# Attention in units of half the sequence of a pair of heads, and a dense expert whose work starts after four units

## The chip, the cores and the metric

One core of a Trainium2 chip runs the whole program in one launch. The metric is device time in microseconds. The engines are TensorE (PE), VectorE (DVE), ScalarE (ACT), GpSimd (POOL) and SyncE (SP, which here issues DMAs alone). Before the change the median of three runs is 761.54 us (760.5 to 762.2).

## The reference

Two parts follow each other: block attention with sorted keys and values, then a dense mixture of eight experts over its output.

```python
# attention: B=4 batches, H=8 heads, S=768, D=64, 8 blocks of 96 positions
P = sort_net                                  # (B, H, 8, 8)
for _ in range(5):                            # a Sinkhorn iteration
    P = exp(P - max(P, -1)); P /= sum(P, -1) + 1e-9; P /= sum(P, -2) + 1e-9
k_sorted = einsum('bhij,bhjcd->bhicd', P, k_blocks)     # likewise v_sorted
scores = q_block @ k_sorted_block.T / 8       # each block of q sees one block of 96 keys
out = softmax(scores) @ v_sorted_block

# experts: x is (3072, 512), the heads side by side; 8 experts, F = 1024
P = exp(x @ w_gate - max)                     # (3072, 8)
for _ in range(8): P /= sum(P, 1); P /= sum(P, 0); P *= 3072 / 8
out = sum over e of P[:, e] * (relu(x @ w1[e]) @ w2[e])
```

All experts run on all tokens. The routing weights need every token's logits, and so the end of attention; an expert's own product `relu(x @ w1) @ w2` needs only the tokens that it is computed for.

## The kernel before

**Layout.** Matmul operands are bf16, sums f32 in PSUM. A pair of heads n (16 of them, four in a batch) is loaded by `load_pair` as three DMAs from POOL (k, v, q) into the tiles `kvr` and `qr`: each of the 128 partitions holds six neighbouring positions of both heads, so the partition is (block, CH = 16) and the six positions are CL. `relayout` (POOL; for pair 0 `relayout_part` on ACT) brings k and v of a position side by side, for the sort's weights.

**One unit of attention.** There are 32 units, one for each batch and head (NH = 32; unit g belongs to pair g // 2). The functions, which appear below with their lines, are:

- `q_transpose(n)` for a pair: six PE transposes of 128 columns, then four copies into `qT_`, two on DVE and two on ACT (the first two pairs: all four on ACT).
- `build_R` makes a unit's sort matrix R (128 x 8 x 16) from the Sinkhorn result `Pb`, on POOL for two units at a time.
- `sort_kv(g)`: six matmuls of 128 columns, one for each of the six positions in a partition, whose weights are k and v and whose moving operand is R; ACT copies the result to `kvT_` (three buffers), and SP issues a DMA transpose of v's half into `v1_`.
- `scores(g)`: eight matmuls of 96 columns, one for each block; DVE takes the maximum of each row (`mx`) and subtracts it (`ssb`).
- `weights(g)`: ACT's exp into `at_`. For units 16 to 29 (`DT`) a DMA transposes it into `aT_`; for the others `a_transpose` does, with eight PE transposes and a copy on ACT.
- `attend(g)`: eight matmuls of 65 columns (the 65th is the sum of the weights). `normalise(g)`: a reciprocal and a product on DVE, into `og_`.
- `x_transpose(n)` for a pair: eight PE transposes and a copy on ACT into `xtT`, the expert's input with features on the partitions.

`sort_kv`, `scores` and `attend` share two double-bank PSUM buffers (`psB`); the transposes and the expert pieces share four single banks (`psF`).

**Order.** The order of instructions is written out by hand; each engine works its own list in that order. A loop over steps s = 0 to 33 has, in each step: `scores(s)`, `a_transpose(s - 1)`, `sort_kv(s + 2)`, `weights(s)`, in even steps `q_transpose(s // 2 + 1)` and `relayout(s // 2 + 2)`, then any `x_transpose`, then `attend` and `normalise` of the unit before (of two units before, for those whose weights go by DMA), then `load_pair` by a table of steps.

**Expert 0 inside attention.** Between these, at four places in each step, `fill()` puts in pieces of expert 0: `l1_piece` (four matmuls of 384 columns and a Relu on ACT) and `l2_piece` (eight of 512 columns and a copy to the accumulator `osbl`, on DVE or, in one of three from chunk 2 on, ACT). A chunk is 384 tokens: eight l1 pieces and three l2 pieces. A list of slots spreads a batch's two chunks and its gate logits (`gate_piece`) over the calls that follow:

```python
        if new:
            add(new, {9:34,17:40,26:28}[s])
```

A batch is complete after its fourth pair's `x_transpose`, in steps 9, 17 and 26; the last batch's two chunks run after the loop, beside the routing. `load_expert(0)` (w1 and w2, two DMAs on POOL) stands at the end of step 2. Two buffers of `w1e` and two of `w2e` take turns; experts 1 to 7 run after the routing, 3072 tokens each, in groups of 512.

**After the loop** DVE works the routing's Sinkhorn iterations, beginning with the maximum `gmx`, while PE runs the remaining pieces of expert 0 and the first of expert 1, then experts 1 to 7.

Of the kernel before, what the change touches and what calls it, by code (L numbers as in the profile page):

```python
# [24 lines left out]
def kernel(  # L25
# [11 lines left out]
    nc = tc.nc  # L37
# [23 lines left out]
    rawp = ctx.enter_context(tc.tile_pool(name="rawp", bufs=6))  # L61
    iop = ctx.enter_context(tc.tile_pool(name="iop", bufs=2))
    raw_t, kv_t = {}, {}

# [9 lines left out]

    def relayout(n):

        kv = iop.tile([128, 2 * CL, 2, D], BF16, name="kv")
        nc.gpsimd.tensor_copy(kv.rearrange("p c t d -> p t c d"),  # L78
                              raw_t[n][0].rearrange("p t h c d -> p t (h c) d"))
        kv_t[n] = kv  # L80

    def relayout_part(n, e, t):

        if n not in kv_t:
            kv_t[n] = iop.tile([128, 2 * CL, 2, D], BF16, name="kv")
# [6 lines left out]
    load_pair(4)  # L92
# [15 lines left out]
    qT_ = perp.tile([128, 2, 2, S + 32], BF16)  # L108

    def zero_q(a):  # L110
        nc.scalar.copy(qT_[64:128, a].rearrange("p b c -> p (b c)"),
# [3 lines left out]
    nc.vector.memset(qT_[0:64, :, :, S:], 0.0)  # L115
# [45 lines left out]
    wp = ctx.enter_context(tc.tile_pool(name="wp", bufs=2))  # L161
    wg = ones.tile([128, 4, E], BF16)
    w1t, w2t = [], []

    def load_expert(e):
        w1e = wp.tile([128, 4, F], BF16, name="w1e")
        w2e = wp.tile([128, 8, Dm], BF16, name="w2e")
        nc.gpsimd.dma_start(out=w1e, in_=moe_w1[e].rearrange("(kk k) f -> k kk f", k=128))  # L168
        nc.gpsimd.dma_start(out=w2e, in_=moe_w2[e].rearrange("(fb k) f -> k fb f", k=128))
        w1t.append(w1e)  # L170
        w2t.append(w2e)
# [48 lines left out]
    def batch_pieces(b):  # L220

        out_ = []
        for c in (2 * b, 2 * b + 1):
# [29 lines left out]
    def q_transpose(n):  # L253


        qr = raw_t[n][1]
        tq = psF.tile([128, 2, CL // 2, 128], BF16, name="psF")
        for e in range(2):
            for c in range(CL // 2):
                nc.tensor.matmul(tq[:, e, c], qr[:, e, 2 * c:2 * c + 2].rearrange("p l d -> p (l d)"),  # L260
                                 Ibf, is_transpose=True, start=True, stop=True)
        for e in range(2):
            to = qT_[0:64, n % 2, e, 0:S].rearrange(
                "p (i c l h) -> p l c i h", i=NB, l=2, h=CH)
            for l in range(2):
                (nc.vector.tensor_copy if e == 0 and n > 1 else nc.scalar.copy)(  # L266
                    to[:, l], tq[64 * l:64 * l + 64, e].rearrange("p c (i h) -> p c i h", h=CH))

    q_transpose(0)
    q_transpose(1)  # L270


# [289 lines left out]
```

## Time and profile before

| | us |
|---|---|
| median of three runs | 761.54 (760.5 to 762.2) |
| the profiled execution, its own time | 760.26 |
| its span, first to last instruction | 758.5 |
| first sort of keys and values (step 0) | 14.23 |
| first matmul of expert 0 | 53.85 |
| `gmx`, the routing begins | 153.07 |

The span is what the profiler's page counts in; 1.8 us of the execution lie around it. "Busy" is the time in which an engine works on at least one instruction, "idle before" the time that it stood still just ahead of an instruction, with what released it. Matmul ends are modelled, so the spacing of starts tells more of PE than durations do. The mean granted clock of TensorE is 0.993 of full speed.

### The profile page before, as it was taken

The numbers are of one execution on the slowest core, as the hardware profiler recorded it, in microseconds if no ns is written. First come the engines' busy times: TensorE is split into PE (matmuls) and PEld (weight loads), VectorE is DVE, ScalarE is ACT, GpSimd is POOL, SyncE is SP. The second block draws the span as 40 slices with busy tenths as digits, with TensorE's granted clock in tenths as the row PEclk, the third lists the DMA queues.
The fourth block names the chain that finished last, engine by engine and source line by source line (L and its number), as shares of the span: only waits on it lengthen the run. The fifth ranks groups of instructions, "written<-read, shape, count | busy, mean of one in ns | idle before, by whom it ended". The sixth has DMA issues, their size and how long they took to land.

```text
span 758.5 us, 10311 instructions
## 1 busy us (share of the span) xinstructions
PE 725.8 (96%) x4274; PEld 367.7 (48%) x4340; DVE 268.3 (35%) x462; ACT 331.5 (44%) x559; POOL 80.6 (11%) x105
## 2 busy tenths in 40 slices
PE   2779999999999999999999999999999999999998
PEld 2566666654444444444444444444444444444444
DVE  5788787567422122121221221212212212112122
ACT  7888887653433423324324234243242342432422
POOL 8955420000000000000000000000000000000000
PEclk9979999999999999999999999999999999999999
DMA  9999744537000600033000700051001500002112
GB/s 152 191 179 173 101 92 83 80 51 111 1 1 0 102 10 1 0 53 59 0 1 1 111 1 1 0 81 31 0 1 29 83 0 1 1 0 98 70 69 98
DMA packets 58430, 40.14 MB, mean 53 GB/s; under 512 B 30608, under 2 KB 51344, under 8 KB 58384
## 3 DMA queue, kind: packets, MB, share of 16 engines
q0 software_dynamic: 26128, 26.23, 22.8%
q1 hardware_dynamic: 32256, 13.25, 8.4%
q8 instruction: 34, 0.56, 0.3%
q14 instruction: 12, 0.10, 0.0%
HBM read 52.45 MB, written 6.29 MB: 77 GB/s over the span
## 4 chain that ended last, share of the span: by engine, by line
PE 91%; ACT 3%; DVE 3%; DMA 1%; issue 1%; ACTq 0%; DVEq 0%
PE hps L445 38%; PE psF L523 38%; PE psF L203 5%; PE psF L192 5%; DMA v__108<-kvT__106 1%; PE psB L317 1%; PE psB L302 1%; ACT kvT__106 L305 1%; PE psB L346 1%; PE psF L339 1%; DVE ssb L324 1%; ACT at__114 L328 1%; DVE mx L322 0%; ACT qT__111 L266 0%; PE psF L364 0%
## 5 line engine op out<-in xcount | busy, mean ns | idle before, releaser
L448 ACT ACTIVATE hTs<-hps 128x512 bf16<-128x512 f32 x336 | 200.6, 597 | 372.9 <-PE hps L445 365.7
L445 PE MATMUL hps<-xtT,w1e 128*128 128x512 bf16 x1317 | 295.7, 379 | 1.5
L523 PE MATMUL psF<-w2e,hTs 128*128 128x512 bf16 (+1 forms) x1325 | 295.2, 378 | 1.4
L525 DVE SCALAR_TENSOR_TENSOR osbl<-psF,glog,osbl 128x512 f32<-128x512 f32 (+1 forms) x169 | 126.3, 747 | 437.6 <-PE psF L523 425.7
L523 PEld LDWEIGHTS <-hTs 128*128 128x128 bf16 x1352 | 132.2, 98 | 157.9
L445 PEld LDWEIGHTS <-w1e 128*128 128x128 bf16 x1344 | 131.6, 98 | 158.4
L192 PE MATMUL psF<-xtT,w1e 128*128 128x384 bf16 x256 | 49.0, 326 | 0.6 <-ACT qT__111 L266 0.6
L168 POOL DMA_DIRECT2D w1e<-in_moe_w_dram x8 | 6.1, 768 | 394.3 <-PE hps L445 370.4
L203 PE MATMUL psF<-w2e,hTs 128*128 128x512 bf16 x180 | 44.2, 379 | 0.6
L195 ACT ACTIVATE hTs<-psF 128x384 bf16<-128x384 f32 x64 | 29.7, 499 | 7.4 <-PE psF L192 6.8
L322 DVE TENSOR_REDUCE mx<-psB 96x8 f32<-96x768 f32 x32 | 30.4, 949 | 5.8 <-PE psB L317 5.4
L324 DVE TENSOR_TENSOR ssb<-psB,mx 96x768 f32<-96x768 f32 x32 | 30.5, 954 | 3.2
L305 ACT CAST kvT__106<-psB 128x768 bf16<-128x768 f32 x32 | 25.9, 809 | 11.6 <-issue 7.1
L192 PEld LDWEIGHTS <-w1e 128*128 128x128 bf16 x256 | 22.9, 98 | 12.7 <-issue 1.0
L328 ACT ACTIVATE at__114<-ssb 96x768 bf16<-96x768 f32 x32 | 27.3, 854 | 1.8 <-DVE ssb L324 1.8
L203 PEld LDWEIGHTS <-hTs 128*128 128x128 bf16 x192 | 17.8, 100 | 17.0
L78 POOL COPY kv<-kvr 128x1536 bf16<-128x1536 bf16 x15 | 22.0, 1468 | 30.5 <-issue 16.6
L355 DVE TENSOR_TENSOR og__236<-psB,den 96x512 bf16<-96x512 f32 x32 | 22.0, 686 | 1.1
L346 PE MATMUL psB<-v__108,aT__115 97*128 97x65 bf16 x256 | 13.6, 199 | 7.4 <-ACT kvT__106 L305 5.2
L302 PE MATMUL psB<-R,kv 128*128 128x128 bf16 x192 | 18.6, 242 | 1.9 <-ACT kvT__106 L305 0.9
L260 PE MATMUL psF<-Ibf,qr 128*128 128x128 bf16 x96 | 9.7, 248 | 11.0 <-DMA qr<-in_q_dram 11.0
L317 PE MATMUL psB<-kvT__106,qT__111 128*128 128x96 bf16 x256 | 18.0, 219 | 2.2 <-ACT kvT__106 L305 1.5
(82 smaller groups left out, 275.1 us busy)
## 6 DMA issues: line engine op xcount, KB each, us to landing
w1e<-in_moe_w_dram POOLq DMA_DIRECT2D x8, 1024.0 KB, 8.0
w2e<-in_moe_w_dram POOLq DMA_DIRECT2D x8, 1024.0 KB, 8.7
out_dram<-osbl SPq DMA_DIRECT2D x23, 256.0 KB, 2.0
kvr<-in_k_dram POOLq DMA_DIRECT2D x16, 192.0 KB, 7.6
kvr<-in_v_dram POOLq DMA_DIRECT2D x16, 192.0 KB, 7.6
qr<-in_q_dram POOLq DMA_DIRECT2D x16, 192.0 KB, 7.6
v__108<-kvT__106 SPq DMA_TRANSPOSE x32, 4.6
out_dram<-osbl SPq DMA_DIRECT2D x2, 128.0 KB, 1.7
```

The source lines that it names most:

```text
L192: nc.tensor.matmul(hps[:, 0:HC], w1t[0][:, kk, fb * 128:(fb + 1) * 128], xtT[:, kk, c * HC:(c + 1) * HC], start=(kk == 0), stop=(kk == 3))
L195: nc.scalar.activation(out=hT0[c][:, fb, 0:HC], in_=hps[:, 0:HC], func=AF.Relu)
L203: nc.tensor.matmul(oacc, hT0[c][:, fb, tt * 128:(tt + 1) * 128], w2t[0][:, fb, :], start=(fb == 0), stop=(fb == 7))
L302: nc.tensor.matmul(kvf[:, cl * 128:(cl + 1) * 128], kv[:, e * CL + cl].rearrange("p t d -> p (t d)"), R[:, g].rearrange("p i c -> p (i c)" ...
L305: nc.scalar.copy(kvT_[:, g % NKT, :, 0:96].rearrange("p i (l c) -> p i l c", c=CH), mkap(kvps, [kvps.ap[0], [CH, NB], [128, CL], [1, CH]]))
L322: nc.vector.reduce_max(out=mx, in_=s4, axis=AX.X)
L324: nc.vector.tensor_sub(ssb, s4, mkap(mx, [mx.ap[0], [4, 2], [1, 4], [0, 96]]))
L328: nc.scalar.activation(out=at_[:, g % NAT, :, 0:96], in_=ssb_t.pop(g).rearrange("p a i c -> p (a i) c"), func=AF.Exp, scale=scale)
L445: nc.tensor.matmul(hps, w1t[e][:, kk, fb * 128:(fb + 1) * 128], xtT[:, kk, nc4 * 512:(nc4 + 1) * 512], start=(kk == 0), stop=(kk == 3))
L448: nc.scalar.activation(out=hT[e, nc4][:, fb, :], in_=hps, func=AF.Relu)
L523: nc.tensor.matmul(oacc[:, 0:W], hT[e, nc4][:, fb, tt * 128:(tt + 1) * 128], w2t[e][:, fb, c0:c0 + W], start=(fb == 0), stop=(fb == 7))
L525: nc.vector.scalar_tensor_tensor(out=osbl[:, t, c0:c0 + W], in0=oacc[:, 0:W], scalar=glog[:, t, e:e + 1], in1=osbl[:, t, c0:c0 + W], op0=A ...
```

## The change

Attention's unit is no longer one head with its 8 blocks, but one half of the sequence (4 blocks) of both heads of a pair. In a batch the first halves of its four pairs come first, then the second halves. `units[g]` gives (pair, None, half). So:

- After four units the first 384 tokens of a batch have all their features, and chunk by chunk, not batch by batch, the pieces of expert 0 are handed to `fill()`: in steps 5, 9, 13, 17, 22 and 26.
- `sort_kv` works with half of R for each of two heads: twelve matmuls of 64 columns. `q_transpose` is called for each unit, with six matmuls of 64 rows and columns and two copies, on DVE from unit 2 on. `x_transpose` is called for each unit, with four matmuls and a half-size copy on ACT. `unit_R` builds R for each unit on POOL (the first eight heads' first halves on DVE).
- All four pairs of a batch must stay in SBUF until their second halves are sorted. The relaid-out k and v now lie in the second buffers of the expert weights (`kv_tile`), which expert 1 first needs at the end of attention; seven raw pairs are kept for six.
- The order of the loads is written anew: pair 4 is loaded in step 0, no longer ahead of the loop, and w1 and w2 of expert 0 in steps 2 and 4, no longer both in step 2. Pairs 2 and 3 are laid out before step 1.
- `keep_warm(n)` issues n matmuls of 128 columns on the identity into a PSUM buffer that nobody reads: 79 around the start, and ten in each of steps 0 to 4.

The core of the diff:

```diff
-    rawp = ctx.enter_context(tc.tile_pool(name="rawp", bufs=6))
-    iop = ctx.enter_context(tc.tile_pool(name="iop", bufs=2))
+    rawp = ctx.enter_context(tc.tile_pool(name="rawp", bufs=7))
+    wp = ctx.enter_context(tc.tile_pool(name="wp", bufs=2))
+    w1t = [wp.tile([128, 4, F], BF16, name="w1e") for _ in range(2)]
+    w2t = [wp.tile([128, 8, Dm], BF16, name="w2e") for _ in range(2)]
...
+    HALF = (0, 1, 2, 3)
+    QD, AD = range(2, 32), ()
+    units = []
+    for b in range(B):
+        ns = range(4 * b, 4 * b + 4)
+        if b in HALF:
+            units += [(n, None, hf) for hf in range(2) for n in ns]
+        else:
+            units += [(n, e, None) for n in ns for e in range(2)]
...
+    def kv_tile(n):
+        w = (w1t, w2t)[n % 4 // 2][1]
+        return mkap(w, [w.ap[0], [2 * D, 2 * CL], [D, 2], [1, D]], off=n % 2 * 2 * F)
...
     load_pair(3)
-    load_pair(4)
...
-    qT_ = perp.tile([128, 2, 2, S + 32], BF16)
+    qT_ = perp.tile([128, 4, S + 32], BF16)
...
+            tq = psF.tile([128, CL // 2, 2, 64], BF16, name="psF")
+            ps = slice(64 * hf, 64 * hf + 64)
             for c in range(CL // 2):
+                for e in range(2):
+                    nc.tensor.matmul(tq[:, c, e], qr[ps, e, 2 * c:2 * c + 2].rearrange("p l d -> p (l d)"),
+                                     Ibf[ps, ps], is_transpose=True, start=True, stop=True)
+            fr = [tq.rearrange("p c e (i h) -> p c (e i) h", h=CH)]
+        for e, f in enumerate(fr):
+            to = qT_[0:64, (u + e) % 4, 0:S].rearrange(
                 "p (i c l h) -> p l c i h", i=NB, l=2, h=CH)
             for l in range(2):
+                dve = e == 0 if hf is None else l == 0 or u in QD
+                (nc.vector.tensor_copy if dve and u > 1 else nc.scalar.copy)(
+                    to[:, l], f[64 * l:64 * l + 64])
+    def keep_warm(n):
+        w = psF.tile([128, 512], F32, name="psF")
+        for i in range(n):
+            nc.tensor.matmul(w[:, (i % 4) * 128:(i % 4 + 1) * 128], Ibf, Ibf, start=True, stop=True)
+    keep_warm(32)
     q_transpose(0)
+    keep_warm(28)
     q_transpose(1)
...
+            for a in (range(2) if e is None else (e,)):
+                r = R[:, 2 * n + a] if hf is None else R[:, 2 * n + a, 4 * hf:4 * hf + 4]
+                w = 128 if hf is None else 64
+                o = cl * 128 + (0 if hf is None else 64 * a)
+                nc.tensor.matmul(kvf[:, o:o + w],
+                                 kv[:, a * CL + cl].rearrange("p t d -> p (t d)"),
+                                 r.rearrange("p i c -> p (i c)"), start=True, stop=True)
...
-    build_R(nc.vector, Pps, 0, 2)
+    build_R(nc.vector, Pps, 0, 4, 0, 4)
     nc.vector.tensor_copy(Pb, Pps[:, 0:256].rearrange("p (i g) -> p i g", g=32))
     sort_kv(0)
-    build_R(nc.gpsimd, Pb, 2, 2)
+    build_R(nc.vector, Pps, 4, 4, 0, 4)
+    keep_warm(10)
     relayout(1)
-    load_pair(5)
+    relayout(2)
...
-    loads = {2 * n - 11: n for n in range(6, 11)}
-    loads.update({10: 11, 11: 12, 13: 13, 15: 14, 17: 15})
+    loads = {0: [4], 1: [5], 3: [6], 5: [7], 8: [8], 9: [9], 10: [10], 11: [11], 13: [12], 14:[13],15: [14], 18: [15]}
     new = []
     for s in range(NH + 2):
-        if s % 2 == 0 and s + 4 < NH:
-            build_R(nc.gpsimd, Pb, s + 4, 2)
+        if s == 0:
+            relayout(3)
+        if s + 4 < NH:
+            unit_R(s + 4)
...
         fill()
+        if s < 5:
+            keep_warm(4)
...
+        if s + 2 < NH and units[s + 2][1] != 1:
+            q_transpose(s + 2)
+        for n in range(4, NP):
+            if first[n] == s + 4:
+                relayout(n)
+        for g in x_step.get(s, []):
+            x_transpose(g)
+            n, e, hf = units[g]
             if n % 4 == 3 and n < NP - 1:
...
+                    new = batch_pieces(n // 4, (hf,))
+                    if hf == 1:
+                        new.insert(0, (0.7, gate_piece(n // 4)))
         fill()
+        if s < 5:
+            keep_warm(6)
...
         if new:
-            add(new, {9:34,17:40,26:28}[s])
+            add(new, {5: 16, 9: 18, 13: 18, 17: 18, 22: 20, 26: 28}[s])
             new = []
         if s == 2:
-            load_expert(0)
+            load_w1(0)
+        if s == 4:
+            load_w2(0)
```

## The prediction, made before the changed kernel ran

> **What bounds the kernel now.** First the page, for where TensorE (PE) is not full.
>
> ```profile
> span 758.5 us, 10311 instructions
> ...
> PE 725.8 (96%) x4274; PEld 367.7 (48%) x4340; DVE 268.3 (35%) x462; ACT 331.5 (44%) x559; POOL 80.6 (11%) x105
> ...
> PE   2779999999999999999999999999999999999998
> ```
>
> PE is the bound, and only the first three slices (57 us) lack work. The window sums, cut at step 0's first sort, at step 5, 11, 18, 28 and 31's `mx` (VectorE, DVE), and at `gmx`, where the routing starts, show how much:
>
> ```profile
> 14.23:34.13 19.90, 14.32 (x182) 12.21 (x181) 14.40 (x24) 14.98 (x23) 19.53 (x27) 1.00 1.31 194
> 34.13:57.26 23.13, 17.33 (x252) 15.12 (x253) 18.39 (x32) 18.77 (x29) 14.00 (x17) 0.78 1.30 181
> 57.26:86.83 29.57, 28.58 (x334) 19.83 (x336) 23.32 (x37) 25.15 (x45) 15.51 (x18) 1.00 1.08 149
> 86.83:126.11 39.28, 37.40 (x451) 25.68 (x455) 33.84 (x58) 31.19 (x55) 8.36 (x9) 1.00 0.51 86
> 126.11:140.60 14.49, 14.14 (x140) 9.12 (x140) 10.09 (x17) 9.98 (x19) 0.00 (x0) 1.00 0.41 69
> 140.60:153.07 12.47, 12.42 (x133) 7.78 (x133) 5.88 (x12) 7.57 (x14) 1.84 (x3) 1.00 0.69 116
> 153.07:758.50 605.43, 599.34 (x2770) 276.27 (x2823) 153.24 (x244) 212.45 (x359) 9.81 (x12) 1.00 0.17 33
> ```
>
> Columns: stretch, length, busy time (and instructions) of PE, of its weight loads, of DVE, of ScalarE (ACT) and of GpSimd (POOL), granted clock, DMA share, GB/s. From `mx` of step 5 to `gmx` are 118.94 us with PE busy 109.87, so idle 9.07, of which 5.80 in steps 5 to 10, before any expert piece exists; there the clock is 0.78. From step 11 on PE is at 95 to 99%, DVE at 79, 86, 70 and 47%. What lies after `gmx` isn't touched. Next, the groups by line and shape (busy us, mean ns, idle before), for what one instruction costs:
>
> ```profile
> L322 DVE TENSOR_REDUCE mx<-psB 96x8 f32<-96x768 f32 x32 | 30.4, 949 | 5.8 <-PE psB L317 5.4
> ...
> L302 PEld LDWEIGHTS <-kv 128*128 128x128 bf16 x192 | 14.6, 109 | 5.7 <-issue 1.5 <-DVE og__236 L355 0.9
> ...
> L266 ACT COPY qT__111<-psF 64x384 bf16<-64x384 bf16 x36 | 17.0, 471 | 0.3
> ...
> L367 ACT COPY xtT<-psF 128x768 bf16<-128x768 bf16 x16 | 12.7, 794 | 0.1
> ...
> L266 DVE COPY qT__111<-psF 64x384 bf16<-64x384 bf16 x28 | 9.8, 351 | 1.5 <-PE psF L260 1.3
> ```
>
> Last, PE's timeline in step 4 (start, us), for what narrow matmuls cost at full clock, and the longest piece of the chain that ended last:
>
> ```profile
> 30.99 0.50 PE L302 MATMUL psB<-R,kv 128*128 128x128 bf16 x6
> 31.33 0.50 PE L260 MATMUL psF<-Ibf,qr 128*128 128x128 bf16 x6
> 32.72 0.40 PE L346 MATMUL psB<-v__108,aT__115 97*128 97x65 bf16 x8 [0.90 <-ACT aT__115 L341]
> 32.96 0.51 PE L317 MATMUL psB<-kvT__106,qT__111 128*128 128x96 bf16 x8
> ```
>
> ```profile
> 32.77 10.65 DMA v__108<-kvT__106
> ```
>
> Starts tell the spacing: six of 128 columns take 0.34 us (56 ns each), eight of 65 columns, each with its own weight load, 0.24 (30 ns). The piece of the chain explains steps 5 to 10: `kvT_` has three buffers, each held by a copy (0.8) and v's transpose, 11.45 us for three steps, or 3.8 each, and they took 23.13/6 = 3.85. (With pieces a step takes 4.2, which covers it.)
>
> **The change, part by part.** Pieces: six chunks of expert 0 run inside attention before and after. The first now exists after unit 3's `x_transpose` (step 5) and runs from step 6, no longer from the end of step 10 (its first matmul at 53.85 us). The work is the same; what can be won is PE's idle time in steps 6 to 10, and it shows as less left to drain after step 26 (12.42 of 12.47 us in the 140.60 row).
>
> PE's own work. `sort_kv`: 12 matmuls of 64 columns for 6 of 128: 12 x 30 = 0.36 us for 0.34. `q_transpose`: 0.18 us in each step for 0.34 in every second. `x_transpose` has the same eight matmuls for two units. That is +0.03 us a step, +0.9 for the 27 steps from step 5 on. `keep_warm`'s 129 matmuls all stand before step 5. The 69 ahead of the first sort take 3.9 us at 56 ns, or 7.4 at the 107 ns that six in 0.64 us show at half clock, and fit between `Ibf` (4.0 us) and `Pc` (12.7) around q transposes that wait for q at 8.8 and 11.8. The other 60, 3.4 us, meet 5.58 us of idle in steps 0 to 4 (14.23 row). I cost them at nothing; standing in PE's order they delay whatever is ready behind them, at worst 0.56 us a step, 2.8 in all.
>
> Clock. Thirteen groups between 37.56 and 47.95 us run at half clock, each some 0.27 us longer: 3.5 us of PE time. With pieces there PE is busy as in the rows at clock 1.00. I take all 3.5 (step 5, without pieces or warmers, is the risk: then nothing).
>
> DVE. `q_transpose`'s copies go to DVE: two in every unit for two in every second. From step 5 on that is 26 more x 0.351 = 9.1 us, and its busy 91.5 us (sum of five rows) becomes 100.6. The second early `build_R` (0.42) falls into its 2.2 us of idle ahead of the first `mx`.
>
> ACT. 32 copies fewer x 0.471 = -15.1. `xtT` becomes 32 half copies; 384 columns cost between half of 794 and the 499 ns of the 128x384 Relu, so +0 to +3.3. It is lighter by 12 to 15 us, credited at nothing, since it bounds no stage.
>
> POOL and the loads. Same R elements in twice as many instructions, same relayouts; relayout 1 no longer waits behind the loads of pair 4 and an R. k, v and q land about 1 us apart, pair 3's v at 16.5 us; relayouts 2 and 3 end by 15.1 and 18.0, units 2 and 3 are sorted at about 18.2 and 21.3. That holds by three microseconds each. `Pc` at 12.7 stays; the first `mx` gains 0.3 from a sort and scores at full clock. Steps 0 to 4 get three more pairs of q copies on DVE, 2.1 us, beside 5.5 idle: between 0 and +2.1, and I take 0, since until step 2 DVE idles 1.0 to 1.4 before it gets scores or outputs. From relayout 4 on POOL waits for PE's sort of the same slot, two steps before the pair's own sort at the latest. SP issues the same transposes in the same order.
>
> The weights. From relayout 3's end at 18.0, with an issue at 0.72, an R at 0.33 and a relayout at 1.47, POOL issues w1 at about 24 us, pair 6, then w2 at about 29, then pair 7. Now w1 lands 9.5 us after its issue, w2 7.4 after w1, and a pair takes about 4 beside them. That gives w1 at 33.5 (first use about 37), w2 at 44.9 (first L2 piece in step 8, about 45.2: step 6 at 36.8 and two of 4.2), pair 7 at 48.9, relayout 7 at 50.4 (sorted in step 9, about 51). All hold, by little.
>
> Sum. PE's need from step 5 to `gmx`: 109.9 + 0.9 - 3.5 = 107.3. Step 5 has no piece: 3.7 us for 1.6 of work. The other 105.7 at 95.2%, the rate of the 86.83 row, where DVE too was most loaded: 111.0. Together 114.7 for 118.94, so -4.2; with the 0.3 at the start -4.5. The profiled execution took 760.26 us (span 758.5 and 1.8 around it), 1.3 under the median of 761.54; so 755.8 profiled and **757.0** as a median.
>
> **A rule against this change.** The Trainium skill, in "TensorE: Matmul & The Clock Gate", section "LDWEIGHTS (loading the stationary operand)", has a weight load cost its columns over 1.2 GHz whatever the rows: an estimate of 107 ns each, or 31 us for the 288 loads that the split sorts and q transposes add. The trace agrees on the length of one (98 to 113 ns) but not on it as a bound, as eight loads pass in 0.24 us.
>
> **The rivals.**
> A, the forecast: 757.0 (754.5 to 759.5). For it: the stages' 95 to 99%.
>
> B, PE fills better: ACT's relief shortens the waits for copies, and the rate is the 97.6% of the 126.11 row: 105.7/0.976 + 3.7 = 112.0, so 754.3; with no idle left at all 752. Against it: DVE then has 90% of the stretch.
>
> C, slower: DVE becomes the bound. From `mx` 5 to `mx` 31 it is busy 85.6 of 106.47 us, idle 0.80 in each of 26 steps. It gets 9.1 us of copies and two accumulator copies (1.4) that now fall behind `mx` 31: 96.1. The chain from there is `mx` and `ssb` 2.0, exp 0.85, transpose and its copy 1.35, attend 0.4, three normalises 2.6, `x_transpose` and its copy 1.0, gate and copy 1.0: 9.2. Without idle 105.3; every 0.1 of idle a step adds 2.6. It decides above 0.52 a step; there nothing is won, since pieces moved forward only leave holes behind. If the copies fill no idle time and all 0.80 stays: 126.1, so +7.2, 768.7; at 0.65, 764.8. For it: L2 pieces of 1.73 us stand in PE's order ahead of scores and attend. Against it: in steps without q copies DVE now idles 1.1 to 1.5 at a stretch waiting for attend, just where the new copies stand.
>
> D, weights late: pieces wait in PE's own order, so attention stands still behind them. Each microsecond of w2 past 45.2 costs one. Transposes of v take 10.65 us beside the loads, and 4 to 5 us of lateness would leave 761.
>
> E, narrow matmuls bound by their weight loads: 192 x 109 and 96 x 113 ns, 31.8 us, 788. Against it: the 30 ns spacing.
>
> **How the numbers follow.** A 0.46, B 0.17, C 0.22, D 0.11, E 0.04. 0.2% is 1.5 us, about what measuring this kernel can tell. Faster by more: nearly all of A, all B, a little of D: 0.65. Within it: the lower idle of C, half of D: 0.13. Slower: the rest of C and D, and E: 0.22. The range from B without idle to C at 0.65 is 752 to 765.
>
> **What would show it.** Right: `gmx` near 148.6, the first expert matmul near 37, granted clock 1.00 from 37 to 57, twelve sort matmuls within 0.4 us, DVE at 85 to 88% between `mx` 5 and `gmx`. Wrong: DVE idle over 0.5 a step while PE waits for `og` or `ssb` (C); PE waiting for w1, w2 or POOL's relayout in steps 6 to 9 (D); sorts of 1.2 us (E); or half clock in steps 6 to 10, which takes 3.5 off the gain.

## The result, and the profile after

The changed kernel takes 766.38 us (median of four, 765.59 to 767.08) against 761.87 for the kernel before on the same chip: 1.006 of its time, 95% interval 1.0039 to 1.0081. It is slower, where 757.0 was forecast and 765 was the top of the range. The profiled execution took 765.59 us, its span is 763.5 (before: 760.26 and 758.5).

The page first: PE's share of the span is higher than before, not lower, and the slices that lacked work are fuller.

```profile
span 763.5 us, 11243 instructions
...
PE 740.8 (97%) x4757; PEld 376.1 (49%) x4757; DVE 281.2 (37%) x495; ACT 319.7 (42%) x543; POOL 82.2 (11%) x118
...
PE   5799999899999999999999999999999999999998
```

The window sums of the changed kernel, cut at the same events as those of before (first sort, `mx` 5, 11, 18, 28, 31, `gmx`); columns as before: stretch, length, busy time of PE, PEld, DVE, ACT, POOL, granted clock, DMA share, GB/s.

```profile
16.45:38.47 22.02, 16.51 (x306) 14.48 (x304) 16.55 (x30) 13.53 (x19) 17.33 (x27) 0.89 1.12 150
38.47:65.95 27.48, 27.15 (x364) 19.60 (x363) 22.43 (x41) 19.88 (x34) 15.05 (x21) 0.87 1.23 158
65.95:96.00 30.05, 30.02 (x403) 20.82 (x401) 25.77 (x45) 22.87 (x43) 14.82 (x21) 1.00 1.01 140
96.00:136.57 40.57, 39.10 (x544) 26.43 (x541) 36.65 (x67) 27.81 (x49) 9.90 (x14) 1.00 0.48 91
136.57:146.46 9.89, 8.99 (x127) 6.47 (x128) 9.38 (x18) 7.07 (x13) 0.00 (x0) 1.00 0.52 88
146.46:158.02 11.56, 9.26 (x110) 5.67 (x109) 5.89 (x13) 5.96 (x12) 1.89 (x3) 1.00 0.62 103
158.02:763.50 605.48, 602.28 (x2826) 276.01 (x2823) 153.28 (x244) 212.44 (x359) 9.81 (x12) 1.00 0.17 33
```

What lies behind `gmx` is unchanged (605.48 for 605.43). All of the difference lies before it, and these rows beside the earlier ones give its parts:

| part | forecast, us | measured, us |
|---|---|---|
| up to the first sort | -0.3 | +2.22 (16.45 for 14.23) |
| first sort to `mx` 5 | 0 | +2.12 (22.02 for 19.90) |
| PE's work, `mx` 5 to `gmx` | -2.6 (107.3 for 109.87) | +4.65 (114.52) |
| PE's idle there | -1.7 (7.4 for 9.07) | -4.04 (5.03) |
| sum, as forecast rounded | -4.5 | +4.95 |

So the early pieces do fill PE's idle time, and better than forecast. The 4.04 us are given back in three places, 8.99 us in all: the start is later, the steps before 5 are longer, and PE has more work, not less. (Ten of 144 layer-2 matmuls have no record in the trace of before, though their weight loads have; its busy time is some 0.5 us too low by that, an estimate from the holes of 0.05 us that they leave.)

**The start.** DVE's timeline of the changed kernel ahead of the first sort (start, us), then GpSimd's:

```profile
10.62 1.19 DVE L167 TENSOR_TENSOR P<-P,cs 32x64 f32<-32x64 f32 x1
...
13.38 1.39 DVE L167 TENSOR_TENSOR Pc<-P,cs 32x64 f32<-32x64 f32 x1
```

```profile
10.24 1.46 POOL L100 COPY w1e<-kvr 128x1536 bf16<-128x1536 bf16 x1
13.18 1.47 POOL L100 COPY w2e<-kvr 128x1536 bf16<-128x1536 bf16 x1 [1.49 <-DMA kvr<-in_v_dram]
```

Both multiplies begin while a relayout runs, and end 0.11 and 0.12 us after it (11.81 for 11.70, 14.77 for 14.65). In the kernel before the same two take 0.26 us each, since its first relayout stands behind the Sinkhorn. `Pc` is done at 14.77 us instead of 12.7.

**Steps 4 to 7.** From the chain of waits through steps 4 to 6 of the changed kernel (start, us, what), and PE's timeline for the attend in it:

```profile
24.26 11.78 DMA v__107<-kvT__105
...
36.99 0.60 PE psB L406 x8
...
41.75 1.28 PE psF L216 x4
```

```profile
36.99 0.60 PE L406 MATMUL psB<-v__107,aT__114 97*128 97x65 bf16 x8 [2.84 <-ACT kvT__105 L364]
```

Unit 3's transpose of v lands 11.78 us after its issue, PE stands still for 2.84 us, and behind that it runs at half clock until 45.8 us: the first expert pieces take 1.28 us, not 0.65. The stretches at half clock behind `mx` 5, in the kernel before and in the changed one (length, PE busy, clock, DMA share, GB/s):

```profile
37.44:47.68 10.24, 8.64 (x97) 0.50 1.30 178
```

```profile
38.47:45.82 7.35, 7.21 (x77) 0.50 1.29 170
```

At half speed 8.64 us of busy time are some 4.3 us of work lost, 7.21 are 3.6 (estimates).

**Every step.** PE's timeline in step 10, at full clock:

```profile
62.56 0.51 PE L361 MATMUL psB<-R,w1e 128*128 128x64 bf16 x12 [0.20 <-DVE og__300 L419]
63.00 0.34 PE L295 MATMUL psF<-Ibf,qr 64*128 64x64 bf16 x6
63.28 0.34 PE L429 MATMUL psF<-Ibf,og__300 96*128 96x96 bf16 x4
```

From start to start the sort takes 0.44 us and q's transposes 0.28, where 0.36 and 0.18 were forecast.

### The profile page after: what moved, and what is told of

It is laid out like the page before. It is cut to its first block, busy times and chain, and to the rows that moved or that the text cites. A ratio compares the mean times of both kernels' runs of the same rounds, so it can differ in the third digit from the quotient of the medians.

```text
span 763.5 us, 11243 instructions
## 1 busy us (share of the span) xinstructions
PE 740.8 (97%) x4757; PEld 376.1 (49%) x4757; DVE 281.2 (37%) x495; ACT 319.7 (42%) x543; POOL 82.2 (11%) x118
## 4 chain that ended last, share of the span: by engine, by line
PE 92%; DVE 5%; DMA 2%; ACT 1%; issue 0%; DVEq 0%; ACTq 0%
PE psF L609 38%; PE hps L531 38%; PE psF L216 5%; PE psF L227 5%; DMA v__107<-kvT__105 2%; PE psB L361 1%; PE psB L376 1%; DVE og__300 L419 1%; PE psF L429 1%; PE psB L406 1%; DVE ssb L383 1%; PE psF L295 1%; DVE mx L381 1%; PE psF L398 1%; ACT kvT__105 L364 1%
## 5 line engine op out<-in xcount | busy, mean ns | idle before, releaser
L216 PE MATMUL psF<-xtT,w1e 128*128 128x384 bf16 x256 | 51.6, 332 | 0.2
L303 DVE COPY qT__110<-psF 64x384 bf16<-64x384 bf16 x60 | 21.0, 350 | 3.6 <-PE psF L295 3.1
L400 ACT COPY aT__114<-psF 97x768 bf16<-97x768 bf16 x18 | 14.4, 798 | 8.6 <-PE psF L398 8.5
L376 PEld LDWEIGHTS <-qT__110 128*128 128x128 bf16 x256 | 14.4, 101 | 3.8 <-DVE ssb L383 0.8
```

The source lines that it names most:

```text
L216: nc.tensor.matmul(hps[:, 0:HC], w1t[0][:, kk, fb * 128:(fb + 1) * 128], xtT[:, kk, c * HC:(c + 1) * HC], start=(kk == 0), stop=(kk == 3))
L376: nc.tensor.matmul(sps[:, i // 4, (i % 4) * 96:(i % 4 + 1) * 96], qT[:, i * BL:i * BL + 128], kvT[:, i, 0:96], start=True, stop=True)
```

## The experiments

Theory: these three, added up, are the miss. Rivals: one cause behind all of the start (the loads), or the narrow matmuls as such. Each kernel is the changed one with the edit shown, and ran beside the kernel before, whose median was 761.3 to 762.0. "Step 8" is the start of `mx` 8: 52.62 us in the changed kernel, 45.85 before, where it stands for other work.

### The start: relay

```diff
     keep_warm(10)
+    unit_R(4)          # waits for Pb; skipped in step 0
     relayout(1)
     relayout(2)
```

> Edit: GpSimd builds R of unit 4, which waits for Pb, before the relayouts of pairs 1 and 2, so that both relayouts run behind the Sinkhorn instead of beside it. Theory A (a SBUF-to-SBUF DVE multiply stands still until a GpSimd copy is done): the two multiplies by cs that took 1.19 and 1.39 us take 0.26 us again, Pc is done near 12.7 us instead of 14.8, the first sort is near 14.3 us instead of 16.45, and the time falls by about 2.1 us, to 764.3 (763.5 to 765). Theory B (the first 16 us are longer because of the added filler matmuls or the loads, and the two long multiplies only wait for something that is late anyway): first sort stays near 16.4, time 766.4. The relayouts end later (pair 1 near 16.5 us, pair 3 near 20), which sort 1, at about 18 us, should just not feel.

765.17 us. DVE's timeline of this run:

```profile
10.61 0.26 DVE L167 TENSOR_TENSOR P<-P,cs 32x64 f32<-32x64 f32 x1
...
12.44 0.26 DVE L167 TENSOR_TENSOR Pc<-P,cs 32x64 f32<-32x64 f32 x1
```

Theory A holds for the start: both multiplies are short again and the first sort is at 14.27 us. It fails for the time: step 5 begins at 33.54 us, 4.9 earlier than in the changed kernel, and step 8 at 52.20, only 0.4 earlier. Two waits take it back. PE stands still 2.95 us for the kvT copy, in step 5 instead of 4, and then for w1:

```profile
PE psF L216 <- DMA w1e<-in_moe_w_dram: 1.8, 1, 1.8
```

The loads stand behind the relayouts on GpSimd's queue. With these later, w1 is issued at 25.30 us for 23.29 and lands at 40.81 for 37.09. So this edit moves the loads too, and is no test of the first sort alone.

### What holds step 8: nkt4, w1early, late, spread

```diff
-    NKT, NVB = 3, 5
+    NKT, NVB = 4, 5                      # nkt4
```

> Edit: four buffers for kvT instead of three. In step 4 of the changed kernel the kvT copy waits 3.03 us for the DMA transpose of v of unit 3, which reads the buffer, and PE then idles 2.84 us. Theory A (the transpose itself is late, at 36.0 us, because the loads share the DMA engines with it): attend(3) in the same step needs that v too, so the wait only moves to attend, which can begin at 36.1 instead of 37.0: 0.9 us gained at most, 765.5 (764.5 to 766.5). Theory B (the third buffer is what is missing): the whole stall of 2.8 us goes and the clock stays up: 763 or less.

764.19 us, first sort at 15.44 (with the relayouts where they are it fell anywhere from 14.6 to 16.8 in the runs, by which multiply met a copy: by `cs`, 1.25 us in nkt4 and 1.44 and 1.45 in spread; by `rs`, 0.56 in late and 1.52 in qpair, always to about 0.1 us after the copy's end). The wait moved to attend as theory A has it: 1.4, 0.85 and 1.65 us in steps 2, 4 and 5, each ending 0.14 us after v of the unit has landed. 2.2 us are won; how much of that comes from the first sort, 1.0 earlier, is not shown.

```diff
     nc.gpsimd.dma_start(out=wg, ...)
+    load_w1(0)                           # w1early; w2 in step 2 instead of 4
```

> Edit: expert 0's w1 is loaded straight behind the gate's weights (issue near 15.4 us instead of 23.3), w2 at the end of step 2 instead of step 4 (near 23.3 instead of 28.4). Theory A (w1 and the pair loads issued between 23 and 28 us crowd the DMA transposes of v of units 2 to 4): those of units 3 and 4 land within 10.5 us instead of 11.8 to 12.9, step 4 has no stall, the clock does not fall at 36 us, and the time is 2 to 3 us shorter, 763.9 (763 to 765). Theory B (the DMA engines are full from 16 us on, and order only moves the stall): v of units 0 to 2 land later instead, a stall of 2 to 3 us stands in steps 1 to 3, time 766 to 768.

765.46 us, between the ranges of the two theories. For the stall theory B holds: v of units 0 to 2 now land 9.9 to 12.2 us after issue, a stall of 4.5 us stands in step 1 (`mx` 2 at 28.6 us for 25.1), units 3 and 4 take 9.0 and 9.1, and step 8 is at 52.18.

```diff
-                    new = batch_pieces(n // 4, (hf,))
+                    # late: both halves of batch 0 from step 9, slots 32, 32, 32, 28, 28
...
-        if s == 2:
+        if s == 5:
             load_w1(0)
-        if s == 4:
+        if s == 7:
             load_w2(0)
```

> One part of the change undone: expert 0's pieces begin at step 9 with both halves of the first batch (22 pieces and the gate) instead of at step 5 with the first half; w1 is loaded at the end of step 5 and w2 of 7 instead of 2 and 4; the filler matmuls go on to step 8; slots 32, 32, 32, 28, 28. Theory A (early pieces are worth what they fill, 8.7 us of PE work in steps 5 to 8, but their loads cost the stall and the low clock, 6 to 7 us): steps 0 to 8 run at 3.4 to 3.6 us each at full clock, step 9 begins near 50 us instead of 58.2, the 8.7 us of pieces come back in the full steps behind it, and the time is within 2 us of the changed kernel: 766 (764.5 to 768). Theory B (early pieces fill nothing, steps are as long with them as their PE work): 4 us or more shorter. Theory C (their loads cost nothing): 6 to 8 us longer.

765.99 us, the time of theory A, but not by its way: step 9 begins at 52.52 us, not near 50. The stall went where w1 went. The chain of waits of this run names the same transfer three steps later, and PE's waits show what it cost:

```profile
33.41 12.39 DMA v__107<-kvT__105
```

```profile
PE psB L406 <- ACT kvT__105 L364: 4.4, 2, 3.4
```

(us in total, times, longest.) It is unit 6's v that is late, not unit 3's; those of 3, 4 and 5, now without w1, take 9.8, 9.6 and 6.7 us, and step 4 keeps a stall of 1.0. Without early pieces the kernel is no faster and no slower, though its first sort is at 14.62 us, 1.8 earlier, and fillers run to step 8: what the pieces fill and what their loads cost are about equal, to a microsecond or two.

```diff
-    loads = {0: [4], 1: [5], 3: [6], 5: [7], ...}
+    loads = {0: [4], 1: [5], 4: [6], 6: [7], ...}   # spread; w2 in step 7
```

> Edit: pair 6 is loaded at the end of step 4 instead of 3, pair 7 at the end of 6 instead of 5, w2 at the end of 7 instead of 4; w1 as in the changed kernel. Theory A (pair 6 and then w2 in flight beside w1 are what makes v's transposes take 12 to 13 us): v of unit 3 lands 8 to 10 us after its issue instead of 11.8, v of units 4 to 6 in 7 to 9, no stall in step 4, the clock stays up, and the time is 4 to 6 us shorter, 761.5 (760 to 763.5). Theory B (w1 alone delays them as much): 11 to 12 us for unit 3, stall and clock as before, 765 to 767. What could go wrong: pair 7 or w2 come late, and steps 9 to 11 wait for sort(11) or the first layer-2 piece.

772.77 us. v of unit 3 still takes 11.8: theory B, in so far as w2 is not needed for it. That w1 alone is enough is not shown, since pair 5 was in flight beside it until 30.8 us and pair 6 from 28.2. And PE waited 5.1 us for w2:

```profile
PE psF L227 <- DMA w2e<-in_moe_w_dram: 5.1, 1, 5.1
```

### The order of the loads: early45, early45b

```diff
     load_pair(3)
+    load_pair(4)
...
     relayout(1)
+    load_pair(5)       # early45; in early45b behind relayout(2)
     relayout(2)
...
-    loads = {0: [4], 1: [5], 3: [6], ...}           # w1 in step 1 instead of 2
+    loads = {2: [6], ...}
```

> Edit: the loads of pairs 4 and 5 go back ahead of the relayouts on GpSimd's queue (4 right behind 3, 5 between relayouts 1 and 2, as in the kernel before), pair 6 at the end of step 2, w1 at the end of step 1; w2 and pair 7 as in the changed kernel. Theory A (what holds step 8 near 52 us in all runs so far, 50.9 to 52.6, wherever the first sort was, is the data in flight: the DMA queue is nearly empty from 15.6 to 19 us because pair 4 is issued behind the relayouts): relayout 1 runs near 13.7 us, behind the last long multiply, so the first sort is near 14.3 us; 3 to 4 us of DMA time are won, w1 lands near 33 us, step 8 begins near 49 instead of 52.6, and the time is 3 to 4 us shorter, 762.7 (761 to 764.5). Theory B (what holds it is v's transposes beside any load, and the clock that falls behind the first stall): the stall comes earlier, in step 3, step 8 stays near 52, time 765 to 767.

762.57 us (ratio 1.0015, 1.0003 to 1.0028), step 8 at 48.92: theory A, to 0.1 us in both. It moved 202 and 195 GB/s in the two windows of four microseconds from 14 us on, where the changed kernel moved 118 and 107. Here are the same two windows of early45b (length; busy time of PE, PEld, DVE, ACT and POOL; clock, DMA share, GB/s):

```profile
14.00:18.00 4.00, 3.52 (x49) 3.24 (x47) 2.21 (x5) 1.53 (x2) 4.00 (x5) 0.57 1.31 202
18.00:22.00 4.00, 3.50 (x72) 2.98 (x72) 3.52 (x6) 2.53 (x5) 4.00 (x9) 1.00 1.37 190
```

> early45 with the load of pair 5 behind relayout 2 instead of ahead of it, since sort(2) waited 2.1 us for relayout 2 in early45qa. Theory A (the start is a matter of the order on GpSimd's queue: long multiplies, relayouts, loads): first sort 14.3 us, no wait for a relayout in steps 0 and 1, step 8 near 47.5 us, 761 (759.5 to 763). Rival (v's transposes beside w1 hold the start): the wait comes back at an attend in steps 2 to 4, step 8 at 49 as in early45, 762.5.

762.15 us (ratio 1.0007, 0.9994 to 1.0019). The first sort is at 14.26 and no relayout is waited for, but v takes 9.9 to 11.1 us beside w1, attend(3) waits 1.7 us, and step 8 is at 49.10: the rival.

### The clock and the length of rows: warm4, warmb, chunk, chunkb

```diff
         if s < 5:
-            keep_warm(6)
+            keep_warm(6 if s < 4 else 50)    # warm4; warmb: early45b with 20 in step 3, 36 in step 4
```

> Edit: in step 4, 50 filler matmuls (2.8 us at the full clock) instead of 6 ahead of attend(3), in the 2.84 us in which PE waits there. Theory A (the wait itself costs under 3 us, but the clock that falls to 0.50 behind it for some 9 us costs another 4): the clock stays at 1.00, the first layer-1 pieces take 0.65 us instead of 1.28, and the time is 4 us shorter, 762.4 (761 to 764). Theory B (the stretch to 52 us is set by when the transposes of v and w1 land, and the clock only fills the wait): waits for v or w1 take the place of the slow matmuls, and the time stays within 1 us of 766.4.

765.62 us. The first sort was at 14.72 us, 1.7 earlier; step 4 took the fillers (5.8 us), and the stall of 2.9 us stood in step 5, with the clock at 0.50 behind it (40.8 to 44.8 us); step 8 at 52.63. Theory B, but not a test of the clock.

> early45b with 20 fillers instead of 6 ahead of the attend of step 3 and 36 of step 4, where PE waited 1.7 us for the kvT copy and its clock fell to 0.50 from 34.8 to 41.5 us. Theory A (the stall itself is small, the low clock behind it costs about half of 6.7 us): with the clock kept, the first layer-1 pieces take 0.65 us, step 8 begins near 47 us instead of 49.1, and the time is 2 to 3 us shorter than early45b: 759.6 (758.5 to 761). Rival (the stall moves to a step that has no fillers, or the landing of v holds the steps anyway): step 8 at 49, 762.

762.06 us, step 8 at 49.15: the rival again. This time the low clock (0.63 and 0.52) was at 22 to 30 us, ahead of the fillers. A filler by step number cannot sit on a stall that moves between executions. What the clock costs by itself stays an estimate from the windows.

```diff
-        nc.gpsimd.dma_start(out=w1t[e], in_=moe_w1[e]...)
+        for f in range(0, F, F // 4):        # expert 0 alone: rows of 1 KB, not 4
+            nc.gpsimd.dma_start(out=w1t[e][:, :, f:f + F // 4], in_=moe_w1[e][:, f:f + F // 4]...)
```

> The changed kernel with expert 0's w1 loaded in four column slices (rows of 1 KB instead of 4 KB of f32), all four issued at the end of step 2: same bytes, shorter rows, 2.4 us more of issuing on GpSimd. Theory A (v's transposes take turns with the load row by row, so long rows are what makes them 12 us late beside w1 and 7 to 8 beside the pairs, whose rows are 1.5 KB): v of unit 3 lands 8 to 9 us after its issue, no stall in step 4, 3 to 5 us shorter: 762.4 (761 to 764.5). Theory B (what counts is how many bytes are in flight): 11 to 13 us as before, stall as before, 765.5 to 767.5.

763.38 us, with the first sort at 14.86. v of units 3, 4 and 5 takes 10.2, 9.6 and 8.6 us for 11.8, 12.1 and 12.9, the stall is 1.5 us for 2.84: theory A, but not to the end, as the clock still falls, and a layer-2 piece waits 1.8 us for w2, which is issued later.

```diff
 # chunkb: the edits of early45b and of chunk
```

> early45b with w1 in the same four slices. By Theory A of the slices: v of units 2 to 4 land in 7 to 8 us instead of 9.9 to 11.1, no wait at the attend of step 4, clock 1.00 from 18 us on: 759 (757.5 to 761). By Theory B: as early45b, 762.

761.06 us (ratio 0.9988, 0.9974 to 1.0002), between the two theories. v of units 3 to 5 takes 9.1 to 9.6 us for 9.9 to 11.1 in early45b; that of units 0 to 2, beside pairs 4 and 5 and from 21.5 us the first slices of w1, 8.1 to 9.7, and attend waits 2.0 us for it in step 1. The stall is not gone, it stands elsewhere.

### PE's own work: qpair, probe, q128

```diff
-                    nc.tensor.matmul(tq[:, c, e], qr[ps, e, ...], Ibf[ps, ps], is_transpose=True, ...)
+                    nc.tensor.matmul(tq[:, c, :, e], qr[:, e, ...], Ibf, is_transpose=True, ...)
+        # qpair: once for both halves, in the first half's unit; second half's copies on ACT
```

> Edit: a first half's unit transposes q of the whole pair (6 matmuls of 128 rows and 128 columns for two units, the form of the kernel before) and copies it out for both halves: the first half's by DVE, the second half's by ACT (two extra buffers of qT lie in the gaps of the relaid k and v). Theory A (the narrow matmuls are what PE pays: 6 of 64 rows and 64 columns take 0.28 us for one unit, 6 of 128 take 0.34 for two): 0.11 us of PE a step less, 3.0 us over 27 steps, and 0.35 us of DVE a step less: time 3 to 4 us shorter, 763 (761.5 to 764.5). Theory B (PE waits for DVE in the loop and its own work hides): the gain comes from DVE's part only in steps 18 to 31, where DVE is busy over 90 per cent, 1 to 2 us. Theory C (copies for two units bunched in every first-half step push ACT and DVE): no gain or up to 2 us longer.

763.28 us. From `mx` 11 to `gmx` it takes 90.55 us for 92.07: 1.5 of the 2.2 us that 0.11 a step makes there. But the sort, which was not touched, fell from 0.445 to 0.35 us.

```diff
     q_transpose(1)
+    keep_warm(48)
+    for o, a in probe(A_, 64, 64):               # rows, columns, spacing of the outputs
+        mm(o, a, Ibf[:, 0:64], start=True, stop=True)
+    ...                                          # nine more groups, outputs unread
```

> Added behind q_transpose(1), while PE waits for the Sinkhorn anyway: 48 filler matmuls, then ten groups of 24 matmuls whose stationary operand changes from one to the next (six slices of pair 0's q) and whose moving operand is a slice of the identity; each group on its own line: 128 rows with 64 columns written side by side, the same written 128 apart, 128 rows with 65 columns, 97 rows with 65 columns, 97 rows with 64, 64 rows with 64, 64 rows with 64 as a transpose, 128 rows with 96, with 128, with 128 as a transpose. The time itself says nothing. In the changed kernel the sort (128 rows, 64 columns) takes 37 ns each, the narrow q transposes (64 rows, 64 columns) 47 ns, attend (97 rows, 65 columns) 30 ns. Theory A (the rows of the stationary operand set the floor): 128 rows with 64 or 65 columns 37 ns, 97 rows 30, and 64 rows less still unless it is a transpose. Theory B (fewer rows than 128 do not help, the place of the output does): side by side 37, 128 apart 30. Theory C (what was slow is the stream of which they are part, other instructions between them): all plain narrow groups 27 to 30 ns. For 64 rows: if the form itself is slow, 47 ns in the transpose group.

PE's timeline of the probe, six of its groups of 24:

```profile
14.26 0.86 PE L329 MATMUL psF<-Ibf,qr 128*128 128x64 bf16 x24
14.96 0.86 PE L331 MATMUL psF<-Ibf,qr 128*128 128x64 bf16 x24
...
17.12 0.98 PE L337 MATMUL psF<-Ibf,qr 97*128 97x64 bf16 x24
18.04 0.87 PE L339 MATMUL psF<-Ibf,qr 64*128 64x64 bf16 x24
18.75 0.86 PE L341 MATMUL psF<-Ibf,qr 64*128 64x64 bf16 x24
19.54 1.20 PE L343 MATMUL psF<-Ibf,qr 128*128 128x96 bf16 x24
```

From start to start, 24 take 0.70 us (29 ns each) with 128 rows, and 0.71 with 64: theories A and B fall, C holds for the plain groups. The exceptions are the groups at a change: 97 rows ahead of 64 take 0.92, and the 64-row transposes ahead of 128 rows 0.79. Of the first, only 0.10 us stands at the change, as the end of that group shows; the rest is a pause of 0.13 inside it, whose cause is open:

```profile
17.45 0.66 PE L337 MATMUL psF<-Ibf,qr 97*128 97x64 bf16 x17
18.04 0.20 PE L339 MATMUL psF<-Ibf,qr 64*128 64x64 bf16 x1
```

(17 at 29 ns are 0.49 us, and it is 0.59 to the next group.) Going from plain matmuls of 64 rows to transposes of 64 rows costs nothing (0.71 us). So the forecast's 30 ns was right for each matmul; what it lacked is a price for going from many rows to 64 and back.

```diff
-            tq = psF.tile([128, CL // 2, 2, 64], BF16, name="psF")
+            tq = psF.tile([128, CL // 2, 2, 64], F32, name="psF")
-                    nc.tensor.matmul(tq[:, c, e], qr[ps, e, ...], Ibf[ps, ps], is_transpose=True, ...)
+                    nc.tensor.matmul(tq[:, c, e], qr[:, e, ...], Ibf[:, 64 * hf:64 * hf + 64], ...)
```

> Edit: q_transpose multiplies all 128 rows of q with the 64 columns of the identity that pick the half (a plain matmul into f32 PSUM), instead of transposing the 64 rows of the half; same number of matmuls and of columns. Theory A (a matmul of 64 columns takes 29 ns, and what made 12 of the sort take 0.445 us and 6 of q 0.28 is the change between 128 rows and 64 rows, 0.10 us each way): the sort takes 0.35 us and q 0.18 us, 0.2 us of PE a step less, 4 us over the some 20 steps where PE binds; against it stand the copies from f32, 0.35 us now and perhaps 0.45 to 0.5, two a step on DVE, which is over 90 per cent busy from step 18 on: 2 to 3 us shorter in all, 763.7 (762 to 765.5). Theory B (the narrow columns are the price): sort and q as before, and the dearer copies make it 0 to 3 us longer.

766.76 us. PE's timeline in this run, and DVE's copies in the groups from `mx` 18 to 28:

```profile
103.75 0.51 PE L360 MATMUL psB<-R,w2e 128*128 128x64 bf16 x12
104.10 0.34 PE L294 MATMUL psF<-Ibf,qr 128*128 128x64 bf16 x6
104.28 0.34 PE L428 MATMUL psF<-Ibf,og__300 96*128 96x96 bf16 x4
```

```profile
L302 DVE CAST qT__110<-psF 64x384 bf16<-64x384 f32 x20 | 11.0, 549 | 0.1
```

Theory A for PE: 0.35 and 0.18 us with the same matmul and column counts, so the change of rows costs 0.10 us each way, 0.2 a step. (This edit also turns transposes into plain matmuls; qpair kept the transposes, with 128 rows, and its sort fell by the same 0.10.) From `mx` 5 to 18 the run is 2.3 us shorter than the changed kernel. Then the copies from f32 (549 ns for 349, two a step) put DVE at 40.50 of 42.61 us from `mx` 18 to 28, and the steps to `mx` 31 take 2.9 us more. DVE binds there, as rival C of the forecast described it, once its copies cost more.

### All of it together: early45qa, combo, best, sum

```diff
 # early45qa: the edits of early45 and of q128, and
-                dve = e == 0 if hf is None else l == 0 or u in QD
+                dve = e == 0 if hf is None else l == 0
```

> early45 and q128 together, with every second q copy on ACT. Theory A of both: 3.7 and 4 us, 758.7 (757 to 761). If the start is held by the transposes of v: 762 to 763. If ACT's copies stand in front of the kvT copy: steps of 4 us and more from 18 on, no gain over early45.

761.3 us (ratio 0.9993, 0.9982 to 1.0003): 5.1 less than the changed kernel, 2.6 short of the sum. sort(2) waited 2.1 us for relayout 2, now behind a load; and from `mx` 11 to `gmx` it took 91.77 us for 92.06 in early45: PE's 1.8 us less work there (85.56 for 87.37) left holes.

```diff
 # combo: the edits of early45qa, and
-            add(new, {5: 16, 9: 18, 13: 18, 17: 18, 22: 20, 26: 28}[s])
+            add(new, {5: 16, 9: 18, 13: 18, 17: 18, 22: 20, 26: 22}[s])
```

> early45qa with 22 slots instead of 28 from step 26 on, so that the last layer-2 pieces are out of the way of the last units. Theory: PE has work in 9.26 of the last 11.56 us now, and the units' own chain there is about 9 us; the last stretch is 1 to 2 us shorter and the steps before it up to 1 longer: 758 (756 to 760.5), shorter than the kernel before. Rival: the steps 26 to 31 take up what the last stretch gives: the same time as early45qa.

762.08 us: the rival. In the profiled execution, which at 763.64 us is the slowest of twelve, `mx` 31 is 3.4 us later (145.15) and the last stretch takes 8.64 us for 11.54, but PE idles there and its clock falls. Two windows of it (length, PE busy, clock, DMA share, GB/s):

```profile
150.00:155.00 5.00, 3.24 (x44) 0.71 1.04 172
155.00:160.00 5.00, 5.00 (x21) 0.61 1.19 197
```

What follows `gmx` takes 608.11 us instead of 605.4.

```diff
 # best: the edits of early45b and of qpair, nothing else
```

> early45b and qpair together: q by pair in 128 rows (no change between 128 and 64 rows, a third fewer columns in all than two transposes of a half plus what the change costs), bf16 copies, half of them on ACT. If the terms add up (start: 3.8 us by early45, perhaps 1 more; q: 0.2 us of PE a step, of which qpair showed 1.5 us behind step 11 and early45qa as much): 759 (757.5 to 761), 0.2 to 0.5 per cent shorter than the kernel before. Rival (the start is held by the transposes of v, and a faster loop only waits): 761 to 762.5, no difference from the kernel before.

763.52 us (ratio 1.0025, 1.0014 to 1.0036): the rival, and worse than it said, 1.4 us above early45b alone. PE waits 2.1 us for v at attend in step 1 and 2.0 for the kvT copy in step 4, and step 8 is at 51.45.

```diff
 # sum: the edits of relay, chunk and qpair, and
-    loads = {0: [4], 1: [5], 3: [6], ...}
+    loads = {0: [4], 1: [5], 4: [6], ...}
-        if s == 4:
+        if s == 3:
             load_w2(0)
```

> The changed kernel with the relayouts behind the Sinkhorn (as in relay), w1 in four slices (as in chunk), w2 at the end of step 3 instead of 4 and pair 6 of 4 instead of 3 (chunk waited 1.8 us for w2), and q by pair (as in qpair). If the terms stand side by side: chunk's 3.0, the first sort near 14.3 us (0.6 more than chunk's 14.86), no wait for w2 (1.8), and 1.5 us behind step 11 from q: 6.9 us less than the changed kernel, 759.5 (758 to 761.5), 0.3 per cent shorter than the kernel before. Rival (faster steps at the start only meet the transposes of v earlier, as in best): step 8 near 49 to 51 us, 761 to 763, no difference from the kernel before.

762.15 us (ratio 1.0014, 1.0001 to 1.0027). Step 8 is at 47.15 us, ahead of the rival's 49 to 51, but takes 9.3: pair 6's v lands at 51.1, its relayout and then a sort wait for it (2.0 us), and w2 is late too (0.9).

No version was shown to beat the kernel before; chunkb and early45qa have the lowest medians and are level with it.

## Why the forecast was wrong

**"POOL and the loads", first half.** "`Pc` at 12.7 stays" failed. The relayouts were timed as POOL work that nobody needs early; that a POOL copy holds up a DVE multiply was not in the sum. Term: -0.3 forecast, +2.2 measured, shown by relay. The Trainium skill, "SBUF — State Buffer", section "SBUF: two separate sides", has it: a DVE instruction with two SBUF inputs and a GpSimd instruction that reads SBUF take one shared pair of ports in turn, each for its whole length. The two rows agree, to 0.12 us.

**"The weights", and rival D.** The weights did come late (w1 at 37.1 us for 33.5, since it took 13.8 us and not 9.5 from its issue; w2 at 49.8 for 44.9), but in the changed kernel pieces did not wait for them. (In relay, chunk, sum and spread they did, 0.9 to 5.1 us, as rival D has it.) What waited was attention, for the transposes of v. The forecast had read their 10.65 us in the trace, and step 5 at 3.7 from them, but let them stay as they were while w1 moved up beside steps 2 to 5 and pair 4 moved behind the relayouts. They took 11.8 to 12.9. Shown: late moves the stall with w1. Shorter rows of w1 shorten them: against warm4, whose first sort and w1 stand at the same times to 0.15 us, chunk has 10.2, 9.6 and 8.6 us for 11.4, 14.0 and 13.5 (pair 6 and w2 are issued later in chunk, by 2.2 and 3.9 us, but spread issues them later still and keeps 11.8). Order can do as much: early45 has 9.1, 8.9 and 9.5 with whole rows, where chunkb has 9.1 to 9.6. In early45 step 8 moved by 3.7 us, with the first sort 2.0 us earlier and w1 landing at 32.8 us; in relay, with the first sort as early and w1 at 40.8, by 0.4. Not shown: that any order is free of it. In every run with pieces from step 5, the probe aside, step 8 began between 47.15 and 52.63 us, and the run that began it first lost it in that very step, to the loads that came last.

**"Clock".** The 3.5 us were taken on the ground that PE would be busy. It was, but behind a stall: half clock until 45.8 us, some 3.6 us of work lost where 4.3 were before, so 0.7 won. The forecast named step 5 as the risk and priced it at nothing won, and half clock in steps 6 to 10 as a sign of being wrong; in step 6 it came.

**"PE's own work".** +0.03 us a step was forecast, +0.21 came (sort 0.445 for 0.34, q 0.28 for 0.17 as half of a pair's), or 5.4 us over 25 steps instead of 0.9. (The forecast's 0.9 is 27 steps at 0.03, which makes 0.8; 25 steps from step 5 on have a sort and a q transpose.) Less the 0.7 of the clock that makes 4.7, for 4.65 measured, as far as the half microsecond of missing records lets one say. The number of matmuls and 30 ns for each were right, so rival E falls; the change between row counts was missed because the timeline of before has no group of 64 rows between groups of 128 to read it from.

**Right.** DVE's busy from `mx` 5 to `gmx`: 100.6 forecast, 100.12 measured (five rows), 84% of the stretch, short of the 85 to 88 only because the stretch is longer. Rival C did not decide here, though DVE is near it from `mx` 18 on (36.65 of 40.57): from `mx` 5 to 31 DVE idles 13.8 us, or 0.53 a step, just above C's 0.52, but PE waits only 2.0 us for `og` and `ssb` in all that time. The idle left on PE, 5.03 us, is less than the 7.4 forecast.

The sum of the three failed terms (2.5 and 2.1 at the start, 7.2 of PE work) is 11.8 us, less 2.3 for the idle: 9.5, the difference of the two sums in the table. The first and the third went away when their cause was taken away (relay, q128); the second moved with w1. The versions that take away several are 2.9 to 5.3 us shorter than the changed kernel, not 9.5: their traces show new waits for loads, relayouts and copies, and what each of these costs stays open.

## What to carry to other kernels

Work moved earlier brings its loads with it: before counting what it fills, list every transfer in flight in the steps it moves to, and give the latency of the ones on the path again beside them, not from the trace of before. A new position on GpSimd's queue is to be checked against DVE's instructions at that moment, and a narrower matmul against the shapes of its neighbours, not only its own spacing. Where a stall and a low clock follow a late transfer, look for where the stall goes when one step is cured: in relay, w1early, late, warm4 and chunkb it moved to another step.

## What the runs showed of the hardware

- A DVE multiply with two SBUF inputs waited for a GpSimd copy to end: 1.19 and 1.39 us for 0.26. The reductions and reciprocals in the same copies' time kept their 0.19 to 0.27.
- Matmuls of 64 columns take 29 ns with 128 or 64 rows (0.70 and 0.71 us for 24); going from 128 or 97 rows to 64, and from 64 to 96 or 128, costs 0.10 us each way, in the kernel as in the probe.
- A DMA transpose of v took 2.5 to 4 us with little beside it and 5 to 14 us among loads of pairs and weights; those over 12 us all ran beside w1 or w2.
- PE's clock can fall behind an idle time of 1.71 us: in early45b it was 1.00 up to 34.6 us, 0.56 over the next 3.4 and 0.50 over the 3.5 after, though PE was busy. The Trainium skill, "TensorE: Matmul & The Clock Gate", section "What's actually happening", has it fall after an idle window of some 3.4 us; here half of that was enough, and in sum 1.43 us (34.09 to 35.52; clock 0.50 from 35.66 to 39.07). The windows of early45b that show it:

```profile
32.30:34.05 1.75, 0.04 (x1) 1.00 1.27 190
34.05:34.60 0.55, 0.55 (x16) 1.00 1.29 190
34.60:38.00 3.40, 3.25 (x47) 0.56 1.24 199
38.00:41.50 3.50, 3.50 (x23) 0.50 1.35 147
```
